# Two raw weight blocks fetched into the x buffer, later loads moved behind the first tile's last layout: a fused linear-attention and two-MLP kernel

## Chip, cores and metric

One core of a Trainium2 chip. The metric is the device time of one execution in microseconds (us). An execution is also given by its span, from the first to the last instruction of the profile.

## What is computed

Linear attention with a decaying state over 4 batches, 8 heads, 768 steps and head size 48, then two MLPs over the 3072 tokens of width 384:

```python
for t in range(S):
    state = alpha[:, :, t, :, None] * state + np.einsum('bhd,bhe->bhde', k[:, :, t], v[:, :, t])
    y[:, :, t] = np.einsum('bhd,bhde->bhe', q[:, :, t], state)
...
h = x @ w_in                                       # 384 -> 2048
g = np.maximum(h, 0.0) + alpha * np.minimum(h, 0.0)
x = g @ w_out                                      # 2048 -> 384
...
a = x @ w1                                         # 384 -> 1024
b = x @ w2
h = a * b @ w3                                     # 1024 -> 1024
return h @ w_out                                   # 1024 -> 384
```

## The kernel before

**Precision.** Each large product is made of three matmuls: every operand is held as a high part and a low part (`hi`, `lo`), and the product lo times lo is dropped. So a matrix must be split into its two parts before a matmul may read it.

**Weights.** They come as 64-bit words. Block i of 16 (`blocks[i]`, for column block f = i of the first MLP) is fetched by `fetch(i)` (L159) into a buffer `raw`, of which there are two. `convert(i)` (L163) then takes four instructions: `upper` on ScalarE writes the high half of the word to the only `top` buffer; `assemble` on VectorE joins `top` and `raw` to `y`, of which there is one buffer; `copy` on ScalarE writes the high part of weight tile `w` from `y`; a subtraction on VectorE writes its low part. `convert(i)` also issues `upper` of block i + 1, ahead of its own copy. `conv_next` (L182) calls `convert` for the next block and, one step later, `fetch(i + 2)`. The weight tiles are called w_81 (block 0), w_82 (block 1), and so on, in the listings of the order.

**Attention.** 24 chunks of 128 steps; four make one tile of 512 tokens, so there are six tiles T. For chunk n, `load(n)` fetches decays `al` (two buffers) and `qk` (two buffers), `load_v(n)` fetches `v` (three). `prep(n)` runs a scan over the decays and forms `qt` and `kn` (VectorE, with a logarithm and an exponential on ScalarE, L228 and L229, in the one buffer `r`). `chunk(n)` updates the state (`Up`, `sst`) and makes the outputs `yp`, then the masked scores of the next chunk (`scp`, `sc`). `place` (L321) carries the outputs by small DMAs into x in the layout of the MLP, for chunk 3 half of them from ScalarE's queue, half from SyncE's. `xsplit` (L335) splits half a tile of x into its parts. x has two buffers (pool `xp`).

**First MLP.** `G1(T, f)` computes `h` for a tile and a column block: 9 matmuls of 512 columns, and from it on ScalarE `u`, on VectorE `g`, on ScalarE and VectorE the two parts of `gs`. `G2(T, f)`, two steps later (LAG), adds 9 matmuls into three accumulators `acc`.

**What sets the order.** The list `first` (L441) is the program order of the attention of tile 0, with `warm_up` (matmuls on zeros that keep TensorE busy) and a clock `tick` behind each unit; `later(k, fn)` runs fn k ticks on. Behind it comes a loop over (T, f), in which each step calls `G1`, some units of the next tile's attention (`attend`), `conv_next` and `G2`. SyncE's queue follows program order (`manual_schedule`). On the other engines a scheduler moves instructions by priority. Each engine then runs its instructions in the order of the built program. All loads stand in SyncE's queue and share a few completion semaphores in turn, so that an issue also waits until an earlier DMA with its semaphore has landed.

Of the kernel before, what the change touches and what calls it, by code (L numbers as in the profile page):

```python
# [14 lines left out]
I32 = mybir.dt.int32  # L15
# [17 lines left out]
SPT = TA // CH  # L33
# [5 lines left out]
SKEW = 14  # L39
WARM0, WARM, REST = 18, 2, 18  # L40
SETTLE = 5
BEHIND = 400
BLK = 2 * DM
NSP = NJ * (3 * DM + 1024)
# [19 lines left out]
def fused_kernel(ctx, tc, qk, al, vv, wf, ws, m_alpha, ident, maskn, out):  # L64
# [58 lines left out]
    def later(k, fn):  # L123
        due.setdefault(clock[0] + k, []).append(fn)
# [6 lines left out]
    raw = {}  # L131
    top = ap1.tile([128, BLK], I32, name="top")

    def words(src, p):
        n = src.shape[1]
        t = p.tile([128, n, 2], I32, tag="raw", name="raw", bufs=2)
        sp.dma_start(out=t.bitcast(I16).rearrange("p n c -> p (n c)")[:, :4 * n - 1], in_=src.bitcast(I16)[:, 1:])
        return t

# [16 lines left out]
    blocks = [wf[f].rearrange("p o c -> p (o c)") for f in range(NF)]  # L156
    blocks += [ws[:, c:min(c + BLK, NSP)] for c in range(0, NSP, BLK)]

    def fetch(i):  # L159
        if i < len(blocks):  # L160
            raw[i] = words(blocks[i], cp)

    def convert(i, last=False):  # L163
        t = raw.pop(i)
# [17 lines left out]
    def conv_next(last=False):  # L182
        i = nconv[0]
        nconv[0] += 1
        if i < len(blocks):
            assert i + 1 in raw or i + 1 == len(blocks)
            convert(i, last)
            later(1, lambda: fetch(i + 2))

    st = {}  # L190

# [9 lines left out]
    def load_v(n):  # L201
        if n >= NSTEP:
            return
        b, c = divmod(n, NC_B)
        v = st["v", n] = ap2.tile([128, H, DP], F32, tag="v", name="v", bufs=3)
        sp.dma_start(out=v, in_=vv[b, c])

    def prep(n, last=False):
        if n >= NSTEP:
            return  # L210
        t = st.pop(("qk", n))
        P = albuf[n % 2]
        flatP = P.rearrange("p a t -> p (a t)")
        scan = dve.tensor_tensor_scan(out=flatP, data0=flatP, data1=scan1.rearrange("p a t -> p (a t)"),  # L214
                                      initial=0.0, op0=ALU.mult, op1=ALU.max)
        if last:
            tc.keep_in_program_order(scan)
        pool.memset(P[:, :, 0:1], 0.0)
        Pv = P[:, :, 1:]
        qt = ap2.tile([128, NP, CH], F32, tag="qt", name="qt")  # L220
        dve.tensor_tensor(out=qt, in0=t[:, 0], in1=Pv, op=ALU.mult)
        r = ap2.tile([128, NP, CH], F32, tag="r", name="r", bufs=1)
        kn = ap2.tile([128, NP, CH], F32, tag="kn", name="kn")
        pend = ap2.tile([128, NP, 1], F32, tag="pend", name="pend")
        pool.tensor_copy(out=pend, in_=P[:, :, CH:])
        st["pend", n], st["qt", n], st["kn", n] = pend, qt, kn

        act.activation(out=r, in_=Pv, func=AF.Ln)  # L228
        act.activation(out=r, in_=r, func=AF.Exp, scale=-1.0)  # L229
        dve.tensor_tensor(out=kn, in0=t[:, 1], in1=r, op=ALU.mult)  # L230
        dve.tensor_tensor(out=r, in0=Pv, in1=r, op=ALU.mult)
        dve.scalar_tensor_tensor(out=kn, in0=r, scalar=2.0, in1=kn, op0=ALU.subtract, op1=ALU.mult)
# [15 lines left out]
    def kT(n, w):  # L248
        if n >= NSTEP:
            return  # L250
        kn = st.pop(("kn", n))
        if ends(n):
            return
        ps = bank([128, NP, 128], "kTp", w)
        for p in range(NP):
            pe.transpose(ps[:, p], kn[:, p], idn)  # L256
        t = ap2.tile([128, NP, 128], F32, tag="kT", name="kT", bufs=1)
        copy(t, ps)
        st["kT", n] = t

    def scores(n, w):
        if n >= NSTEP:
            return
        kn, qt = st["kn", n], st["qt", n]
        ps = [bank([128, NP, CH], "scp", w) for _ in range(2)]
        for p in range(NP):
            for hh in range(2):
                r = slice(64 * hh, 64 * hh + D)
                mm(ps[hh][:, p], kn[r, p], qt[r, p], start=True, stop=True)
        for hh in range(2):  # L270
            sc = ap2.tile([128, NP, CH], F32, tag="sc", name="sc")
            dve.tensor_tensor(out=sc, in0=ps[hh], in1=msk.to_broadcast([128, NP, CH]), op=ALU.mult)  # L272
            st["sc", n, hh] = sc
# [66 lines left out]
    def chunk(n, w, more=True):  # L340
        untie()
        state(n, w)
        yout(n, w)
        if more:
            scores(n + 1, w)
        load_v(n + 3)

    def attn_units(T):
        w = T % 2
# [57 lines left out]
    with tc.manual_schedule(engines={mybir.EngineType.SP}):  # L407
# [18 lines left out]
        def warm_up(n):  # L426
            ps = pab.tile([128, 512], F32, tag="h", name="wu")
            for _ in range(n):
# [9 lines left out]
        dve.tensor_scalar(out=sgn, in0=alpha, scalar1=1.0, scalar2=-2.0, op0=ALU.is_gt, op1=ALU.mult)  # L438
        dve.tensor_scalar(out=sgn, in0=sgn, scalar1=1.0, scalar2=None, op0=ALU.add)
        dve.tensor_tensor(out=salpha, in0=alpha, in1=sgn, op=ALU.mult)  # L440
        first = [lambda: scores(0, 0), lambda: kT(0, 0), lambda: chunk(0, 0), lambda: kT(1, 0), lambda: prep(2),  # L441
                 lambda: (load(4), chunk(1, 0)), lambda: kT(2, 0), lambda: prep(3),
                 lambda: (load(5), chunk(2, 0)), lambda: kT(3, 0), lambda: conv_next(True), lambda: xsplit(0, 0, 2),
                 lambda: chunk(3, 0, False), lambda: (warm_up(REST), conv_next(True)), lambda: (prep(4, True), load(6)),
                 lambda: xsplit(0, 2, 2)]
        for u in first:
            u()
            warm_up(WARM)
# [331 lines left out]
```

## Time and profile before

| | us |
|---|---|
| median of 3 runs | 859.57 (857.78 to 859.61) |
| the profiled execution | 856.45 |
| its span | 854.7 |
| TensorE busy (matmul) | 834.7, 98% of the span |
| VectorE busy | 459.5 |
| ScalarE busy | 352.6 |
| mean granted clock of TensorE | 0.994 |

The shares are means over stages. Attention of tile 0 takes the first 32 us, the change lies between 20 and 90 us, and from about 90 us on the first MLP and all that follows it run with TensorE busy all the time until the last few microseconds. Times are counted from the start of the span.

### The profile page before, as it was taken

How to read it: one execution, taken by the hardware profiler on the slowest of the kernel's cores; microseconds unless marked ns; L12 is line 12 of the kernel's file. 1: busy time of each engine (PE TensorE's matmuls, PEld its weight loads, DVE VectorE, ACT ScalarE, POOL GpSimd, SP SyncE). 2: the span in 40 equal slices, each digit the busy share in tenths (PEclk: the TensorE clock that was granted, in tenths of full speed). 3: DMA queues.
4: the chain of work that ended last, by engine and by line, in shares of the span. 5: the costliest groups of instructions: out<-in, count | busy, mean ns of one | idle time of the engine just before them, and what ended most of it. 6: DMA issues, size and time to landing. Idle time of an engine off the chain costs nothing.

```text
span 854.7 us, 11911 instructions
## 1 busy us (share of the span) xinstructions
PE 834.7 (98%) x4772; PEld 686.0 (80%) x4776; DVE 459.5 (54%) x643; ACT 352.6 (41%) x538; POOL 11.1 (1%) x53
## 2 busy tenths in 40 slices
PE   7899999999999999999999999999999999999996
PEld 4577888888888888888888889988888888888884
DVE  7899876665685586656335634552434435322221
ACT  3567665434454545454335534522223232221221
POOL 0000000000000000000000000000000000000000
PEclk9999999999999999999999999999999999999998
DMA  7667572321673385525003306420302203010001
GB/s 279 221 202 248 181 257 97 105 79 39 227 254 106 129 297 184 184 108 196 3 18 111 123 1 224 141 79 1 134 14 74 74 25 124 1 38 1 37 1 41
DMA packets 49104, 99.56 MB, mean 116 GB/s; under 512 B 4880, under 2 KB 25488, under 8 KB 49040
## 3 DMA queue, kind: packets, MB, share of 16 engines
q1 hardware_dynamic: 48800, 98.62, 34.0%
q8 instruction: 39, 0.64, 0.3%
q14 instruction: 25, 0.20, 0.1%
q10 hardware_dynamic: 240, 0.10, 0.0%
HBM read 75.63 MB, written 18.35 MB: 110 GB/s over the span
## 4 chain that ended last, share of the span: by engine, by line
PE 91%; DVE 4%; ACT 2%; issue 1%; DMA 1%; ACTq 0%; DVEq 0%; SPq 0%
PE ab L372 23%; PE h L372 21%; PE acc L372 11%; PE acc L397 8%; PE acc L398 7%; PE acc L400 7%; PE yp L237 4%; PE w L372 4%; PE scp L237 2%; PE Up L237 1%; PE kTp L256 1%; DMA al<-in_al_dram 1%; DVE al L214 1%; DVE w L151 1%; DVE sc L272 1%
## 5 line engine op out<-in xcount | busy, mean ns | idle before, releaser
L372 PE MATMUL h<-x,w 128*128 128x512 f32 x864 | 213.8, 391 | 3.5 <-ACT x L72 3.0
L372 PE MATMUL ab<-x,w 128*128 128x512 f32 x864 | 203.6, 389 | 0.0
L372 PEld LDWEIGHTS h<-x,w 128*128 128x128 f32 x864 | 161.3, 188 | 37.9 <-ACT x L72 3.5
L372 PEld LDWEIGHTS ab<-x,w 128*128 128x128 f32 x864 | 162.1, 188 | 33.6
L397 PE MATMUL acc<-gs,w 128*128 128x512 f32 x288 | 115.4, 401 | 0.0
L398 PE MATMUL acc<-gs,w 128*128 128x512 f32 x288 | 113.1, 393 | 0.0
L576 DVE TENSOR_TENSOR c<-ab,a 128x512 f32<-128x512 f32 x48 | 33.1, 690 | 145.3 <-PE ab L372 145.3
L384 ACT ACTIVATE u<-h,sgn 128x512 f32<-128x512 f32 x96 | 65.5, 682 | 108.0 <-PE h L372 107.8
L386 DVE SCALAR_TENSOR_TENSOR g<-h,salpha,u 128x512 f32<-128x512 f32 x96 | 71.7, 747 | 68.1 <-ACT u L384 67.7
L372 PE MATMUL acc<-cs,w 128*128 128x512 f32 x432 | 105.8, 389 | 0.0
L389 DVE SCALAR_TENSOR_TENSOR gs<-g,sgn,gs 128x512 fp32r<-128x512 f32 x96 | 71.9, 749 | 51.1 <-ACT gs L388 51.0
L372 PEld LDWEIGHTS acc<-cs,w 128*128 128x128 f32 x432 | 81.0, 188 | 17.2 <-DVE cs L579 0.4
L388 ACT ACTIVATE gs<-g,sgn 128x512 fp32r<-128x512 f32 x96 | 69.1, 719 | 54.0 <-DVE g L386 54.0
L400 PE MATMUL acc<-gs,w 128*128 128x512 f32 x288 | 81.4, 391 | 0.0
L72 ACT ACTIVATE a<-ab 128x512 f32<-128x512 f32 x48 | 28.8, 599 | 109.9 <-PE ab L372 109.9
L72 ACT ACTIVATE cs<-c 128x512 fp32r<-128x512 f32 x48 | 30.2, 629 | 93.4 <-DVE c L576 93.4
L397 PEld LDWEIGHTS acc<-gs,w 128*128 128x128 f32 x288 | 54.4, 189 | 12.4 <-issue 0.2
L400 PEld LDWEIGHTS acc<-gs,w 128*128 128x128 f32 x288 | 54.5, 189 | 11.6
L398 PEld LDWEIGHTS acc<-gs,w 128*128 128x128 f32 x288 | 54.5, 189 | 10.7
L72 ACT ACTIVATE top<-raw 128x768 f16<-128x768 bf16 (+1 forms) x39 | 41.8, 1071 | 29.6 <-DMA raw<-in_ws_dram 20.8
L579 DVE TENSOR_TENSOR cs<-c,cs 128x512 fp32r<-128x512 f32 x48 | 33.2, 691 | 30.8 <-ACT cs L72 30.8
L146 DVE SCALAR_TENSOR_TENSOR y<-raw,top 128x768 int32<-128x768 int32 (+1 forms) x39 | 36.9, 947 | 7.1 <-DMA ws_d<-y 4.5
(64 smaller groups left out, 656.9 us busy)
## 6 DMA issues: line engine op xcount, KB each, us to landing
raw<-in_ws_dram SPq DMA_DIRECT2D x22, 767.8 KB, 5.1
qk<-in_qk_dram SPq DMA_DIRECT2D x24, 512.0 KB, 5.7
raw<-in_wf_dram SPq DMA_DIRECT2D x16, 767.8 KB, 4.7
ws_d<-y SPq DMA_DIRECT2D x22, 384.0 KB, 3.0
al<-in_al_dram SPq DMA_DIRECT2D x24, 256.0 KB, 4.8
v<-in_vv_dram SPq DMA_DIRECT2D x24, 256.0 KB, 4.0
alx<-in_al_dram SPq DMA_DIRECT2D x8, 768.0 KB, 4.7
x_d<-x1e SPq DMA_DIRECT2D x18, 256.0 KB, 4.3
```

The costliest lines, as they stand in the source:

```text
L72: act.activation(out=out, in_=in_, func=AF.Copy)
L146: return dve.scalar_tensor_tensor(out=y, in0=t[:, :, 0], scalar=13, in1=z[:, :n], op0=ALU.logical_shift_right, op1=ALU.bitwise_or)
L237: ins = pe.matmul(*a, **k)
L372: pe.matmul(ps, w, x, start=first and i == 0, stop=last and i == n - 1)
L384: act.activation(out=u, in_=ps, func=AF.Identity, scale=sg)
L386: dve.scalar_tensor_tensor(out=gt, in0=ps, scalar=sa, in1=u, op0=ALU.mult, op1=ALU.max)
L388: act.activation(out=s[:, 0], in_=gt, func=AF.Identity, scale=sg)
L389: dve.scalar_tensor_tensor(out=s[:, 1], in0=gt, scalar=sg, in1=f32(s[:, 0]), op0=ALU.mult, op1=ALU.subtract)
L397: pe.matmul(acc[T][m], r_out[f][:, 0, c], s[:, 0], start=f == 0, stop=False)
L398: pe.matmul(acc[T][m], r_out[f][:, 1, c], s[:, 0], start=False, stop=False)
L400: pe.matmul(acc[T][m], r_out[f][:, 0, c], s[:, 1], start=False, stop=f == NF - 1)
L579: dve.tensor_tensor(out=s[:, 1], in0=c, in1=f32(s[:, 0]), op=ALU.subtract)
```

## The change

Blocks 2 and 3 of the raw weights get a home of their own: a tile `early` in the x pool, which is x's second buffer before tile 1 needs it. They are fetched while chunks 1 and 2 run. Blocks 4 and 5 go to the `raw` buffers of blocks 0 and 1, with the fetch four ticks behind the conversion. A third block is converted in `first`; the preparation of chunk 4 moves to its end, behind the second half of x. The loads of chunk 5 and of v for chunk 6 move behind the placing of chunk 3.

```diff
+BEFORE = 4
...
-    def words(src, p):
+    def words(src, p, t=None):
         n = src.shape[1]
-        t = p.tile([128, n, 2], I32, tag="raw", name="raw", bufs=2)
+        if t is None:
+            t = p.tile([128, n, 2], I32, tag="raw", name="raw", bufs=2)
...
+    early = xp.tile([128, 2, BLK, 2], I32, tag="x", name="early")
+
     def fetch(i):
         if i < len(blocks):
-            raw[i] = words(blocks[i], cp)
+            raw[i] = words(blocks[i], cp, early[:, i - 2] if i in (2, 3) else None)
...
-            later(1, lambda: fetch(i + 2))
+            if i not in (2, 3):
+                later(BEFORE if i < 2 else 1, lambda: fetch(i + 4 if i < 2 else i + 2))
...
-        load_v(n + 3)
+        if n != SPT - 1:
+            load_v(n + 3)
...
-        first = [lambda: scores(0, 0), lambda: kT(0, 0), lambda: chunk(0, 0), lambda: kT(1, 0), lambda: prep(2),
-                 lambda: (load(4), chunk(1, 0)), lambda: kT(2, 0), lambda: prep(3),
-                 lambda: (load(5), chunk(2, 0)), lambda: kT(3, 0), lambda: conv_next(True), lambda: xsplit(0, 0, 2),
-                 lambda: chunk(3, 0, False), lambda: (warm_up(REST), conv_next(True)), lambda: (prep(4, True), load(6)),
-                 lambda: xsplit(0, 2, 2)]
+        first = [lambda: scores(0, 0), lambda: kT(0, 0), lambda: chunk(0, 0), lambda: (kT(1, 0), fetch(2)), lambda: prep(2),
+                 lambda: (load(4), chunk(1, 0)), lambda: kT(2, 0), lambda: (prep(3), fetch(3)),
+                 lambda: chunk(2, 0), lambda: kT(3, 0), lambda: conv_next(True), lambda: xsplit(0, 0, 2),
+                 lambda: chunk(3, 0, False), lambda: (warm_up(REST), conv_next(True), load(5), load_v(6)),
+                 lambda: conv_next(True), lambda: xsplit(0, 2, 2), lambda: (prep(4, True), load(6))]
```

What this does to the order on three engines follows. First ScalarE's queue, from the copy of chunk 3's output (`yT_490` before, `yT_488` now) to the copy that makes the high part of the second half of x (`x<-x`); `r<-al_109` is the logarithm of chunk 4, `w_82` and `w_83` the second and third weight tile. Before:

```order
L72 ACTIVATE yT_490<-yp 128x512
L324 DMA x<-yT_490 48x3x128
L326 DMA x<-yT_490 16x128
L326 DMA x<-yT_490 32x128
L72 ACTIVATE w_82<-y 128x2x384
L228 ACTIVATE r<-al_109 128x512
L229 ACTIVATE r<-r 128x512
L72 ACTIVATE top<-raw 128x768
L72 ACTIVATE x<-x 128x3x256
L72 ACTIVATE w_83<-y 128x2x384
```

And of the change:

```order
L73 ACTIVATE yT_488<-yp 128x512
L329 DMA x<-yT_488 48x3x128
L331 DMA x<-yT_488 16x128
L331 DMA x<-yT_488 32x128
L73 ACTIVATE top<-early 128x768
L73 ACTIVATE w_82<-y 128x2x384
L73 ACTIVATE top<-early 128x768
L73 ACTIVATE w_83<-y 128x2x384
L73 ACTIVATE x<-x 128x3x256
L233 ACTIVATE r<-al_109 128x512
```

Between the last placing DMA and the copy of x stood one weight copy, a logarithm, an exponential and one `top`; now there stand two of `top` and two weight copies, and the logarithm comes after x.

Second, VectorE in the same place, from the low part of w_81 to the low part of x's second half (before) and on to the scan of chunk 4 (now). Before:

```order
L151 TENSOR_TENSOR w_81<-y,w_81 128x2x384
L291 TENSOR_TENSOR sst_112<-tmp,pend 128x256
L146 SCALAR_TENSOR_TENSOR y<-raw,top 128x768
L151 TENSOR_TENSOR w_82<-y,w_82 128x2x384
L214 SCALAR_TENSOR_TENSOR al_109<-al_109,scan_111 128x516
L221 TENSOR_TENSOR qt<-qk,al_109 128x512
L221 TENSOR_TENSOR qt<-qk,al_110 128x512
L230 TENSOR_TENSOR kn<-qk,r 128x512
L231 TENSOR_TENSOR r<-al_109,r 128x512
L146 SCALAR_TENSOR_TENSOR y<-raw,top 128x768
L232 SCALAR_TENSOR_TENSOR kn<-r,kn 128x512
L338 TENSOR_TENSOR x<-x 128x3x256
```

And of the change:

```order
L153 TENSOR_TENSOR w_81<-y,w_81 128x2x384
L148 SCALAR_TENSOR_TENSOR y<-raw,top 128x768
L343 TENSOR_TENSOR x<-x 128x3x256
L153 TENSOR_TENSOR w_82<-y,w_82 128x2x384
L148 SCALAR_TENSOR_TENSOR y<-early,top 128x768
L153 TENSOR_TENSOR w_83<-y,w_83 128x2x384
L343 TENSOR_TENSOR x<-x 128x3x256
L219 SCALAR_TENSOR_TENSOR al_109<-al_109,scan_111 128x516
```

The scan and the products of chunk 4 left the place ahead of x, and the conversion of the third block came into it.

Third, SyncE's queue, from the placing of chunk 2 (`yT_408`) to the load of chunk 6's decays (`al_109`). Before:

```order
L324 DMA x<-yT_408 48x3x128 x2
L326 DMA x<-yT_408 32x128
L326 DMA x<-yT_408 16x128 x2
L326 DMA x<-yT_408 32x128
L137 DMA raw<-in_wf_dram 128x3071
L206 DMA v<-in_vv_dram 128x512
L324 DMA x<-yT_490 48x3x128
L326 DMA x<-yT_490 32x128
L326 DMA x<-yT_490 16x128
L137 DMA raw<-in_wf_dram 128x3071
L197 DMA al_109<-in_al_dram 128x4x128
```

And of the change:

```order
L329 DMA x<-yT_408 48x3x128 x2
L331 DMA x<-yT_408 32x128
L331 DMA x<-yT_408 16x128 x2
L331 DMA x<-yT_408 32x128
L329 DMA x<-yT_488 48x3x128
L331 DMA x<-yT_488 32x128
L331 DMA x<-yT_488 16x128
L202 DMA al_110<-in_al_dram 128x4x128
L203 DMA qk<-in_qk_dram 128x1024
L211 DMA v<-in_vv_dram 128x512
L139 DMA raw<-in_wf_dram 128x3071
```

The raw block and v no longer stand ahead of the placing of chunk 3; chunk 5's loads now stand behind it, and the load of chunk 6's decays is the next row after the last one shown.

## Rows read from the trace of the kernel before

**Rows 1.** The page: its first line, and the busy time of TensorE.

```profile
span 854.7 us, 11911 instructions
PE 834.7 (98%) x4772; PEld 686.0 (80%) x4776; DVE 459.5 (54%) x643; ACT 352.6 (41%) x538; POOL 11.1 (1%) x53
```

**Rows 2.** What TensorE's matmuls waited for in the whole span: total us, times, longest.

```profile
PE h L372 <- ACT x L72: 3.0, 1, 3.0
...
PE scp L237 <- DVE sst L287: 1.3, 1, 1.3
...
PE scp L237 <- DVE tmp L290: 0.6, 1, 0.6
PE h L372 <- DVE x L338: 0.5, 1, 0.5
```

**Rows 3.** The timeline of TensorE: start, duration, line, tiles, shape, count, and the idle time before it with what ended that. `wu` is `warm_up`.

```profile
31.18 1.09 PE L237 MATMUL yp<-qt,sst 64*64 64x128 f32 x16
32.20 5.79 PE L429 MATMUL wu<-zeros 128*128 128x512 bf16 x25
41.00 1.65 PE L372 MATMUL h<-x,w 128*128 128x512 f32 x6 [3.01 <-ACT x L72]
43.15 0.96 PE L372 MATMUL h<-x,w 128*128 128x512 f32 x3 [0.49 <-DVE x L338]
...
61.15 2.20 PE L372 MATMUL h<-x,w 128*128 128x512 f32 x9
```

**Rows 4.** The timeline of ScalarE and of its queue (ACTq: it issues a DMA).

```profile
32.32 0.60 ACT L72 ACTIVATE yT<-yp 128x512 f32<-128x512 f32 x1 [0.77 <-PE yp L237]
32.94 0.73 ACTq L324 DMA_DIRECT2D x<-yT  x1
33.71 1.25 ACTq L326 DMA_DIRECT2D x<-yT  x2
35.00 0.84 ACT L72 ACTIVATE w<-y 128x768 fp32r<-128x768 f32 x1 [2.09 <-DVE y L146]
38.01 0.63 ACT L228 ACTIVATE r<-al 128x512 f32<-128x512 f32 x1 [2.17 <-DVE al L214]
...
39.21 1.05 ACT L72 ACTIVATE top<-raw 128x768 f16<-128x768 bf16 x1
40.13 0.81 ACT L72 ACTIVATE x<-x 128x768 fp32r<-128x768 f32 x1
```

**Rows 5.** The timeline of VectorE.

```profile
33.11 0.95 DVE L146 SCALAR_TENSOR_TENSOR y<-raw,top 128x768 int32<-128x768 int32 x1
35.88 0.96 DVE L151 TENSOR_TENSOR w<-y,w 128x768 fp32r<-128x768 f32 x1 [1.82 <-ACT w L72]
36.76 1.22 DVE L214 TENSOR_TENSOR_SCAN al<-al,scan 128x516 f32<-128x516 f32 x1
...
42.15 0.95 DVE L338 TENSOR_TENSOR x<-x 128x768 fp32r<-128x768 f32 x1
...
64.30 0.96 DVE L151 TENSOR_TENSOR w<-y,w 128x768 fp32r<-128x768 f32 x1
65.30 0.96 DVE L146 SCALAR_TENSOR_TENSOR y<-raw,top 128x768 int32<-128x768 int32 x1
...
82.17 0.42 DVE L287 SCALAR_TENSOR_TENSOR sst<-Up,pend 128x256 f32<-128x256 f32 x1
```

**Rows 6.** The timeline of SyncE's queue; its duration includes the waits inside a group.

```profile
33.21 0.33 SPq L137 DMA_DIRECT2D raw<-in_wf_dram  x1
...
34.81 3.71 SPq L326 DMA_DIRECT2D x<-yT  x2
...
40.90 0.61 SPq L197 DMA_DIRECT2D al<-in_al_dram  x1
```

**Rows 7.** DMA issues in four short stretches (around 33.0, 33.2, 38.0 and 42.3 us): size, and the us from issue to landing.

```profile
x<-yT ACTq DMA_DIRECT2D x1, 72.0 KB, 5.1
...
raw<-in_wf_dram SPq DMA_DIRECT2D x1, 767.8 KB, 4.5
...
x<-yT SPq DMA_DIRECT2D x1, 8.0 KB, 1.8
...
raw<-in_wf_dram SPq DMA_DIRECT2D x1, 767.8 KB, 7.6
```

**Rows 8.** Busy time by stretch: length, then busy time and count of PE, PEld, DVE, ACT and POOL, then TensorE's granted clock (1.00 is full), DMA share and GB/s.

```profile
28.72:82.17 53.45, 48.15 (x365) 36.04 (x364) 49.95 (x69) 36.13 (x52) 3.10 (x9) 1.00 0.63 213
34.00:41.00 7.00, 3.99 (x20) 1.61 (x18) 5.08 (x8) 3.74 (x5) 1.31 (x3) 1.00 0.70 224
...
82.60:87.90 5.30, 5.26 (x28) 4.27 (x28) 5.30 (x8) 2.81 (x4) 0.19 (x1) 0.68 0.95 349
```

**Rows 9.** The timeline of TensorE around the scores of chunk 7.

```profile
80.84 0.48 PE L237 MATMUL scp<-qt,kn 48*128 48x128 f32 x2
82.64 1.16 PE L237 MATMUL scp<-qt,kn 48*128 48x128 f32 x14 [1.32 <-DVE sst L287]
83.73 0.71 PE L397 MATMUL acc<-gs,w 128*128 128x512 f32 x1
...
87.83 1.40 PE L372 MATMUL h<-x,w 128*128 128x512 f32 x5
```

**Rows 10.** The chain of waits: start, duration, what.

```profile
92.20 2.04 PE h L372 x9
```

## The prediction

> **What bounds the kernel now.** I read the page first: TensorE's matmuls fill 834.7 of a span of 854.7 us [rows 1], so the time can only come from the 20 us in which TensorE stands, from filler, or from a low clock. The list of waits then shows where it stands inside the changed stretch: 3.0 us for ScalarE's part of x, 1.3 us for a state update `sst` on VectorE, and two of about half a microsecond [rows 2]. The timeline of TensorE gives them places. Attention of tile 0 ends with the `yp` of 31.18; then come 25 filler matmuls, the wait of 3.01 us, and the first `h` of the MLP at 41.00; the fifth `h` starts at 61.15 [rows 3]. The wait for `sst` lies at 81.32 to 82.64, and what follows runs slowly: from 83.73 to 87.83 TensorE does nine `acc` matmuls and four transposes [rows 9]. Nine matmuls of that size take 2.04 us elsewhere [rows 10], and the transposes, at about 0.1 us each, some 0.4, so 4.10 us stand where 2.45 would do. In that stretch the mean granted clock was 0.68, so for a part of it the clock was at 1.2 instead of 2.4 GHz [rows 8]. Its price was 1.65 us. From 87.83 on TensorE hardly stands, so **the start of that `h`, of block 8, is the finish line**: a microsecond won or lost there is one of the whole kernel.
>
> Who holds the start of the first `h`? ScalarE's queue: placing DMAs until 34.96, the copy of w_82 at 35.00, a logarithm at 38.01 that had waited 2.17 us for a scan on VectorE, `top` at 39.21, and only then x at 40.13 [rows 4]. The landing of the last piece of x is close behind as a second holder. ScalarE's first piece, 72 KB, took 5.1 us, beside a raw block of 768 KB issued 0.27 later and landed after 4.5; the last of SyncE's pieces was held inside a group of 3.71 us [rows 6] and took 1.8 us in itself, from an issue at about 38.0 to a landing at about 39.8 [rows 7]. So the layout was late because of the raw block, but x's copy started 0.3 us after the landing, and `top` stood right ahead of it.
>
> **The placing.** With raw block and v gone from ahead of it, ScalarE's first piece should land about 2 us after its issue at 32.94 (nearest row 1.8, other bound 5.1), at 35.0. SyncE's first piece shares a completion semaphore with it, its third with ScalarE's second piece, so they are issued at about 35.0 and 36.3, and the last lands at about 38.5 to 39.0. That gains roughly 1 us, and I count it at nothing, since ScalarE now comes later than that.
>
> **ScalarE's queue ahead of x.** It now holds two `top` and two weight copies, tied to VectorE at each step. `top` of block 2 starts at 35.00 and gives way after 0.92 [rows 4]; the copy of w_82 takes 0.84, to 36.76; its low part on VectorE starts at 36.8, and the `y` of block 2 follows 1.00 behind it, as the pair at 64.30 and 65.30 does, since there is one `y` [rows 5]; it ends at 38.75. `top` of block 3 may overwrite only then: 38.8; w_83 at 39.7; x at 40.55 for 0.81; the first `h` 0.06 later, at **41.4, which is 0.4 later than now**. The low part of x ends at 42.5, ahead of the seventh matmul, so the 0.49 wait there [rows 3] goes. Two more filler matmuls end at about 38.5 and cost nothing.
>
> **41.4 to 61.** TensorE's order is now three `h` in a row, then the scores of chunk 4. The same work as between 41.00 and 61.15 stands there. Of the waits in it, 0.5 and 0.6 [rows 2] go; new ones are the state update of chunk 4, since its `kT` copy stands in ScalarE's queue behind the logarithm of chunk 5, whose scan comes late (about 1.2 us), and a bank that `g` releases (0.25). Fifth `h`: 41.4 + 20.15 - 1.1 + 1.45 = 61.9, at most 0.8 later than now.
>
> **VectorE decides the end.** From its first `y` at 28.72 to `sst` of chunk 6 at 82.17 it was busy 49.95 of 53.45 us [rows 8], so idle 3.5, of which 1.82 in the opening [rows 5]. The built order now has nearly the same set ahead of that `sst` (a `y` and a `g` more, a `qt` and a `kn` less: +0.3). But it loses more in the opening: 2.5 us for the copy of w_82 (from 34.3 to 36.8), 1.85 for that of w_83 (38.75 to 40.6), and about 1.0 for chunk 3's state and w_81 (estimate, between nothing and the 1.82 of a like wait). That is 5.4 instead of 1.8. The later 1.7 of idle need not come back, as chunk 5's decays land early now; I take 0.3, with 0 and 1.7 as the ends. `sst` then starts at 28.72 + 49.95 + 0.3 + 5.4 + 0.3 = 84.7, against 82.17, and ends at 85.1. TensorE waits for it as before, but with the nine `acc` matmuls of block 5 now ahead of the rest of the scores instead of behind. It reaches the first score of chunk 7 at about 61.9 + (80.84 - 61.15) + 0.45 = 82.0, waits for `kn` until about 83.3 (three VectorE instructions and some 2.1 us before `sst` starts, and 0.7 long), does the seven `acc` left (1.6) to 84.9, and the other scores from 85.15. Those take 7/8 of 1.09 [rows 9], the last transposes 0.35: `h` of block 8 starts at **86.45, against 87.83**.
>
> **The clock** makes the difference. Without its fall before, 87.83 would have been 86.2, and the change loses 0.3. If it stays up now, the change wins 1.4; if it falls again, it loses 0.3. I take that it stays up: dense `acc` work now lies on both sides of the wait. The nearest row is the wait of 3.01 us between filler and `h`, over which the granted clock stayed at 1.00 [rows 8]. A wait of 1.32 us behind small score matmuls was followed by the fall; so the length of a wait alone does not tell, and the other end is kept.
>
> The Trainium skill (TensorE: Matmul & The Clock Gate, Part 1) says that the window over which activity is judged runs freely and is not set back by a kernel, so that the same kernel shows a different count of slow matmuls from run to run. By that rule the fall at 83.7 would belong to one execution and its disappearance would be no gain of the change: the sum would then be +0.3. That is the first rival below. The runs shown neither prove nor exclude it; two of them differ by 1.8 us, which is about the price of one fall.
>
> **Profiled run and median.** The profiled execution took 856.45 us, 1.75 over its span; the median of the runs is 859.57, 3.1 higher. I put the difference on the median: 859.57 - 1.4 = 858.2. What a measurement of this kernel can tell from no change is about 0.2%, 1.7 us, so the forecast itself is *no difference that can be told*.
>
> **Rivals.**
> - *The clock falls again, or its fall is of the run and not of the kernel.* For it: the wait of about 1.3 us for chunk 7 remains. Against: the dense work around it. +0.3, 859.9.
> - *VectorE is no longer the bound.* If its opening idle is 2 us less than I count, `kn` of chunk 7 is ready when TensorE asks, and TensorE runs through: from 82.0 it needs 1.1 for scores, 1.6 for the `acc` left and 0.4 for transposes, so `h` of block 8 starts at 85.1, or at 84.3 if the start of the first `h` also follows the landing (38.7) by more than ScalarE's chain allows. That is -2.7 to -3.5: 856.5. Against it: the dependencies of `top`, `y` and the copies are strict, and each is priced by a row.
> - *Slower: the raw chain.* Decays of chunk 6 are loaded at 40.90 now [rows 6], when the products of chunk 4 let their buffer go. Those products come at about 47.6 in the new order, and the raw block 5 stands behind that load in SyncE's queue: issue at about 49.0, landing with 4.5 to 7.6 us [rows 7] at 53.5 to 56.6. ScalarE's queue blocks on its `top`, ahead of the copy of w_85 and of the next `gs`. The fifth `h` wants w_85 at 61.9, some 3 us behind that `top`; so a landing past about 58.5 delays TensorE one for one. If the loads of chunk 5 and block 4 ahead of it push it to 61, it costs 2.5, and no clock gain is kept: +2.8, 862.3. Against it: at least 2 us of margin.
> - *The change may not do what it says* so far as loads go ahead of the layout; here the built order shows that it does.
>
> **Chances.** Forecast 0.45 (about -0.5 to -2.2, of which 0.15 lies past -1.7 and 0.30 within), clock rival 0.22 (0.17 within, 0.05 past +1.7), TensorE-bound 0.20, raw chain 0.13. So faster 0.35, same 0.47, slower 0.18. The range takes the TensorE-bound case at its near end and some of the slow one: 855.9 to 861.4.
>
> **What would show it.** Right: first `h` at 41.2 to 41.7 with x's landing at 38.5 to 39; VectorE idle over 2 us ahead of w_82's low part; `sst` of chunk 6 two to three microseconds later than 82.17; no stretch at half clock near 84; `h` of block 8 near 86.5. Wrong: a first `h` before 40.5 (the landing was the holder), `h` of block 8 before 85.3, waits for w_85 near 61, or TensorE waits behind 90 us, where I expect none.

## The result: 0.5% slower, and in the first pair of profiles the loss lies behind the predicted finish line

| | before | after |
|---|---|---|
| median of 11 runs each (us) | 858.71 (857.41 to 859.61) | 863.33 (858.88 to 866.39) |
| ratio, with its 95% interval | | 1.0053 [1.0038, 1.0068] |
| profiled execution, its span | 856.45, 854.7 | 862.31, 860.5 |
| mean granted clock of TensorE | 0.994 | 0.992 |

The forecast was 858.2 with a range up to 861.4. The change costs 4.6 us in the median. A second set of twelve runs of the same kernel gave 863.07, ratio 1.0037 [1.0020, 1.0055]. One run of that set took 936.74 us at a granted clock of 0.849, a slow state that two runs of the kernel before also showed (1403.11 and 2158.62); the ratios and the mean clocks below leave these three out.

**What TensorE waits for.** In the list of the kernel after, which answers to [rows 2], the wait for x is as long as before, and the two small waits of the opening are gone. `kn` has three waits of 1.9 in all, the longest, 1.1, near 84, where it had been priced. One line is new: 1.8 us for `x1e`, the copy of a finished accumulator. It stood in no step of the prediction.

```profile
PE h L378 <- ACT x L73: 3.0, 1, 3.0
...
PE scp L242 <- DVE kn L237: 1.9, 3, 1.1
PE scp L242 <- ACT x1e L73: 1.8, 1, 1.8
```

**The opening went as worked out.** ScalarE's timeline of the kernel after answers to [rows 4] (start, duration, line, tiles, shape, count, and in brackets the idle time before it and what ended that). Two pairs of `top` and weight copy stand ahead of x's copy, which starts at 40.45 instead of 40.13.

```profile
34.98 1.07 ACT L73 ACTIVATE top<-early 128x768 f16<-128x768 bf16 x1 [2.11 <-DVE x L343]
35.91 0.82 ACT L73 ACTIVATE w<-y 128x768 fp32r<-128x768 f32 x1
38.80 1.06 ACT L73 ACTIVATE top<-early 128x768 f16<-128x768 bf16 x1 [2.07 <-issue]
39.72 0.82 ACT L73 ACTIVATE w<-y 128x768 fp32r<-128x768 f32 x1
40.45 0.83 ACT L73 ACTIVATE x<-x 128x768 fp32r<-128x768 f32 x1
```

VectorE's timeline answers to [rows 5]: 2.48 us of idle ahead of the low part of w_82, 1.86 ahead of that of w_83 (2.5 and 1.85 were priced), then 0.81 for the `u` of the first `h`, which wasn't priced, and the `sst` of chunk 6 at 85.68.

```profile
36.76 0.96 DVE L153 TENSOR_TENSOR w<-y,w 128x768 fp32r<-128x768 f32 x1 [2.48 <-ACT w L73]
...
40.57 0.96 DVE L153 TENSOR_TENSOR w<-y,w 128x768 fp32r<-128x768 f32 x1 [1.86 <-ACT w L73]
...
45.81 0.75 DVE L392 SCALAR_TENSOR_TENSOR g<-h,salpha,u 128x512 f32<-128x512 f32 x1 [0.81 <-ACT u L390]
...
83.57 0.67 DVE L237 SCALAR_TENSOR_TENSOR kn<-r,kn 128x512 f32<-128x512 f32 x1
...
85.68 0.41 DVE L292 SCALAR_TENSOR_TENSOR sst<-Up,pend 128x256 f32<-128x256 f32 x1
```

TensorE's timeline answers to [rows 3] and [rows 9], and goes on to where the loss is.

```profile
41.33 7.80 PE L378 MATMUL h<-x,w 128*128 128x512 f32 x27 [2.96 <-ACT x L73]
...
62.29 2.20 PE L378 MATMUL h<-x,w 128*128 128x512 f32 x9
...
84.38 0.46 PE L242 MATMUL scp<-qt,kn 48*128 48x128 f32 x2 [1.13 <-DVE kn L237]
...
135.83 1.07 PE L378 MATMUL h<-x,w 128*128 128x512 f32 x4
138.65 0.48 PE L242 MATMUL scp<-qt,kn 48*128 48x128 f32 x2 [1.75 <-ACT x1e L73]
...
139.50 1.74 PE L242 MATMUL scp<-qt,kn 48*128 48x128 f32 x14
...
141.93 1.80 PE L378 MATMUL h<-x,w 128*128 128x512 f32 x4
...
145.65 0.62 PE L378 MATMUL h<-x,w 128*128 128x512 f32 x2
```

The `h` of block 8 starts at 88.08, 0.25 later than in the kernel before. The `h` at 145.65 starts 3.69 later than its fellow, which the next fence shows at 141.96; the loss of 3.44 between them comes in one place. The same matmuls in the kernel before:

```profile
136.57 0.48 PE L237 MATMUL scp<-qt,kn 48*128 48x128 f32 x2
...
137.42 1.16 PE L237 MATMUL scp<-qt,kn 48*128 48x128 f32 x14
...
138.92 1.17 PE L372 MATMUL h<-x,w 128*128 128x512 f32 x4
...
141.96 2.20 PE L372 MATMUL h<-x,w 128*128 128x512 f32 x9
```

Read the pair so: 1.75 us are a wait for `x1e`. From the scores at 138.65 to 145.65 are 7.00 us, from 136.57 to 141.96 only 5.39, and each group inside takes longer (1.74 for 1.16, 1.80 for 1.17): 1.61 us are the clock. A further step of 1.26 comes at about 329, where TensorE waits 0.79 for a late state update, and 0.9 of the 5.9 between the two spans lies behind the last matmul.

**The clock** in the kernel after, by stretch (columns as in [rows 8]):

```profile
28.72:85.68 56.96, 51.78 (x373) 38.22 (x373) 50.02 (x69) 37.02 (x54) 2.78 (x9) 0.97 0.56 192
...
40.00:45.00 5.00, 3.67 (x10) 2.96 (x11) 4.42 (x5) 1.91 (x3) 0.78 (x2) 0.66 0.88 326
82.60:87.90 5.30, 4.17 (x27) 2.96 (x28) 5.30 (x8) 4.13 (x6) 1.23 (x2) 1.00 0.33 101
...
140.00:145.00 5.00, 5.00 (x25) 4.20 (x24) 3.12 (x5) 1.28 (x2) 0.00 (x0) 0.67 0.85 274
```

No half clock near 84, as forecast. But part of 40 to 45, behind the wait for x, and part of 140 to 145, behind the wait for `x1e`, ran at 1.2 instead of 2.4 GHz (granted 0.66 and 0.67 on the mean).

**Where the wait for x1e comes from.** SyncE's queue ahead of the load of chunk 10 (the third chunk of tile 2), in the kernel before:

```profile
122.34 0.33 SPq L178 DMA_DIRECT2D ws_d<-y  x1
122.77 0.37 SPq L137 DMA_DIRECT2D raw<-in_ws_dram  x1
123.19 1.56 SPq L197 DMA_DIRECT2D al<-in_al_dram  x1
```

And after:

```profile
120.26 0.33 SPq L182 DMA_DIRECT2D ws_d<-y  x1
120.69 0.37 SPq L139 DMA_DIRECT2D raw<-in_ws_dram  x1
123.93 0.33 SPq L182 DMA_DIRECT2D ws_d<-y  x1
124.35 0.39 SPq L139 DMA_DIRECT2D raw<-in_ws_dram  x1
124.78 0.91 SPq L202 DMA_DIRECT2D al<-in_al_dram  x1
```

`first` converts three blocks now, and the 16 steps of tile 0 still convert one each: 19 blocks instead of 18 by the end of tile 0. So one more store and one more raw block of 768 KB stand ahead of that load. A store goes out when its block is joined, some 3.7 us apart, so the load is issued 1.59 later. It also takes longer: 7.0 us to landing instead of 5.7 (the DMA view of the two stretches). The scan of chunk 10 on VectorE waits for it, and ScalarE's logarithm (`r<-al`) for the scan. In the kernel before:

```profile
128.96 1.23 DVE L214 TENSOR_TENSOR_SCAN al<-al,scan 128x516 f32<-128x516 f32 x1 [1.05 <-DMA al<-in_al_dram]
...
130.23 0.63 ACT L228 ACTIVATE r<-al 128x512 f32<-128x512 f32 x1 [0.41 <-DVE al L214]
...
135.93 1.55 ACT L72 ACTIVATE x1e<-acc 128x512 f32<-128x512 f32 x3
```

and after:

```profile
131.89 1.23 DVE L219 TENSOR_TENSOR_SCAN al<-al,scan 128x516 f32<-128x516 f32 x1 [1.45 <-DMA al<-in_al_dram]
...
133.16 0.63 ACT L233 ACTIVATE r<-al 128x512 f32<-128x512 f32 x1 [0.95 <-DVE al L219]
...
138.02 1.55 ACT L73 ACTIVATE x1e<-acc 128x512 f32<-128x512 f32 x3
```

The scan of chunk 10 is 2.93 later. Behind it and the logarithm, in VectorE's and ScalarE's order, stand `u`, `g` and `gs` of tile 1 (its column blocks 1 and 2), and behind those, in ScalarE's order, the copies `x1e`. It isn't the accumulators that are late, as some of the expectations below have it: the last `acc` matmul of tile 0 ends at 136.0 in this kernel and at 135.7 in the kernel before. ScalarE comes to copy them only at 138.02 instead of 135.93, and the scores of chunk 8 need one of their banks.

### The profile page after: what moved, and what is told of

It reads as the page before. It is cut to its first block, busy times and chain, and to the rows that moved or that the text cites. A ratio compares the mean times of both kernels' runs of the same rounds, so it can differ in the third digit from the quotient of the medians.

```text
span 860.5 us, 11912 instructions
## 1 busy us (share of the span) xinstructions
PE 838.5 (97%) x4774; PEld 687.8 (80%) x4778; DVE 458.9 (53%) x643; ACT 351.9 (41%) x538; POOL 12.9 (2%) x53
## 4 chain that ended last, share of the span: by engine, by line
PE 81%; DVE 6%; DMA 4%; issue 2%; ACT 1%; SPq 0%; DVEq 0%; ACTq 0%
PE ab L378 23%; PE h L378 18%; PE acc L378 11%; PE acc L403 6%; PE acc L404 6%; PE acc L406 6%; PE w L378 4%; PE yp L242 3%; PE scp L242 2%; DVE y L148 1%; DMA raw<-in_wf_dram 1%; DMA qk<-in_qk_dram 1%; DMA ws_d<-y 1%; PE Up L242 1%; DVE g L392 1%
## 5 line engine op out<-in xcount | busy, mean ns | idle before, releaser
L378 PE MATMUL h<-x,w 128*128 128x512 f32 x864 | 216.1, 393 | 3.0 <-ACT x L73 3.0
L73 ACT ACTIVATE top<-raw 128x768 f16<-128x768 bf16 (+1 forms) x37 | 39.7, 1072 | 31.9 <-DMA raw<-in_ws_dram 20.0
L585 DVE TENSOR_TENSOR cs<-c,cs 128x512 fp32r<-128x512 f32 x48 | 33.2, 692 | 30.9 <-ACT cs L73 30.9
L148 DVE SCALAR_TENSOR_TENSOR y<-raw,top 128x768 int32<-128x768 int32 (+1 forms) x37 | 35.0, 947 | 5.7 <-DMA ws_d<-y 4.6
```

The source lines that it names most:

```text
L73: act.activation(out=out, in_=in_, func=AF.Copy)
L148: return dve.scalar_tensor_tensor(out=y, in0=t[:, :, 0], scalar=13, in1=z[:, :n], op0=ALU.logical_shift_right, op1=ALU.bitwise_or)
L378: pe.matmul(ps, w, x, start=first and i == 0, stop=last and i == n - 1)
L585: dve.tensor_tensor(out=s[:, 1], in0=c, in1=f32(s[:, 0]), op=ALU.subtract)
```

## The experiments

Each ran in twelve runs, x_first_hold in seven, beside the kernel before on the same chip; the ratio is against those.

Theory A: the loss is the late load of chunk 10, from its place behind the extra block. Rivals: it is the changed opening; it is the extra work of converting; it is that all later conversions come one block earlier; it is the clock.

**hold_block.** The change, without the last conversion of tile 0's steps.

```diff
-            if T == 0 or 2 <= T < NTA - 1 and g % 2 == 0:
+            if T == 0 and f < NF - 1 or 2 <= T < NTA - 1 and g % 2 == 0:
```

> The changed kernel with one conversion fewer in the steps of tile 0 (none at the last column block), so that as many raw blocks stand ahead of the load of chunk 10 in SyncE's queue as before the change; the opening stays as changed. Theory A (one raw block and one store more ahead of that load make the scan of chunk 10 late on VectorE, which makes the last g, gs and copies of tile 0's accumulators late): chunk 10's decays land by about 129 instead of 131.8, no wait of TensorE at 137 (1.75 us now) and no low clock behind it, median 858 to 860. Rival B (the new opening itself, with a low clock near 41 in some runs, makes the loss): wait and fall may go, but the median stays at 862 to 864. Rival C (loads are slower throughout tiles 2 and 3): 861 to 862.

858.79 us, ratio 1.0001 [0.9986, 1.0016]. As theory A says: the scan of chunk 10 starts at 126.02, and no wait for `x1e` is left. The opening of the change, which it keeps, makes no difference that can be told (the interval is -1.2 to +1.4 us). That speaks against the opening. But the work is less as well, and later conversions come as in the kernel before; late_block below parts those two.

**before_plus_block.** The kernel before, with one conversion more between the last two steps of tile 0, and with that the extra block alone.

```diff
-            if T == 0 or 2 <= T < NTA - 1 and g % 2 == 0:
-                if T == 0:
+            if T == 0 or (T, f) == (1, 0) or 2 <= T < NTA - 1 and g % 2 == 0:
+                if T <= 1:
```

> The kernel before with one conversion more (between the last two column blocks of tile 0), so that one raw block and one store more stand ahead of the load of chunk 10; the opening is that of before. Theory A: the wait of TensorE near 137 appears, 1 to 2 us, with or without a low clock of 1.7 us behind it, median 861 to 864. Rival B: no wait, 858 to 859.5.

863.18 us, ratio 1.0048 [1.0031, 1.0066]: the whole loss, with the opening of the kernel before. TensorE's timeline of this kernel has the same wait, longer, and the same slow groups behind it:

```profile
133.31 1.07 PE L372 MATMUL h<-x,w 128*128 128x512 f32 x4
138.24 0.48 PE L237 MATMUL scp<-qt,kn 48*128 48x128 f32 x2 [3.86 <-ACT x1e L72]
...
139.38 2.07 PE L237 MATMUL scp<-qt,kn 48*128 48x128 f32 x14
```

**pin_scan.** The change, with the scan of chunk 10 held at its place in the program, so that it can't move ahead of the `g` that it stood in front of.

```diff
-                u += [lambda n=n: prep(n + 2)]
+                u += [lambda n=n: prep(n + 2, n == 2 * SPT)]
```

> The changed kernel with the scan of chunk 10 kept at its place in program order on VectorE, behind chunk 8, so that it no longer stands ahead of the last g of tile 0; the loads are those of the change. Theory A: the late landing (131 to 132) stays, but nothing of tile 0 waits for it: no wait at 137, median 858 to 860.5, with a risk of a wait for chunk 10 further on. If the landing itself slowed TensorE by another way than the scan (ScalarE's top, or a full queue), the wait stays and the median is 862 to 864.

861.43 us, ratio 1.0029 [1.0014, 1.0043], short of what was expected. The wait near 137 is gone, so it went by way of the scan; but the pinned scan also changed VectorE's later order, and a wait of 0.73 for a state update's `tmp` stands at 174 that the change doesn't have. So it doesn't tell how much the late load costs.

**x_first_hold.** hold_block with the second half of x split ahead of the third conversion in `first`, to start the first `h` earlier.

```diff
-                 lambda: conv_next(True), lambda: xsplit(0, 2, 2), lambda: (prep(4, True), load(6))]
+                 lambda: xsplit(0, 2, 2), lambda: conv_next(True), lambda: (prep(4, True), load(6))]
```

> As the first (one conversion fewer ahead of chunk 10's load), and in the opening the split of x's second half put ahead of the conversion of the third block. Theory (ScalarE's queue, not the landing, held the first h): x's copy comes behind one top and one weight copy, so the first h starts when x has landed, at about 39.6 instead of 41.3, and VectorE is less idle; median 856.5 to 859. Rival (landing or VectorE hold it anyway): first h at 41 or later, median as the first.

864.58 us, ratio 1.0050 [1.0026, 1.0074]: a miss. VectorE's timeline shows why. A scan stood ahead of x's low part (43.57) and waited for its decays:

```profile
42.42 1.23 DVE L219 TENSOR_TENSOR_SCAN al<-al,scan 128x516 f32<-128x516 f32 x1 [3.27 <-DMA al<-in_al_dram]
```

The first seven `h` matmuls started at 41.07, the others waited 1.61 for that low part, and `kn` of the next scores came 2.84 late.

**late_block.** The change with all its 19 conversions, the last one four ticks later: on SyncE's queue its store and the next raw block go behind the load of chunk 10. TensorE's order is untouched; on ScalarE and VectorE the `top`, `y`, scan and logarithm between 126 and 133 us change places.

```diff
-                if T == 0:
+                if T == 0 and f == NF - 1:
+                    later(4, conv_next)
+                elif T == 0:
                     conv_next()
```

> As the change, with all 19 blocks converted during tile 0's steps, but the last of them four ticks later, so that its store and the raw block behind it stand in SyncE's queue behind the load of chunk 10 instead of ahead of it. TensorE's order is the same as the change's. Theory A (the load of chunk 10 comes late because of its place in SyncE's queue): no wait for the copy of an accumulator near 137, chunk 10's decays landed by about 129, 858 to 860 us. Theory B (what costs is the work of the extra conversion on VectorE and ScalarE, or the opening of the change): the wait near 137 stays or moves, 862 to 864 us. Theory C (the loss is a clock that falls more often with the change, wherever it waits): no difference to the change, 863.

859.75 us, ratio 1.0016 [0.9997, 1.0035]. The work is the same, later conversions stay one block ahead, only the place differs, and most of the loss is gone: 3.3 to 3.6 us by the medians, 1.8 to 3.2 by the ratios (1.0037 and 1.0053 for the change). The remainder can't be told from nothing. SyncE's queue now shows the load ahead of the last pair:

```profile
121.87 0.63 SPq L202 DMA_DIRECT2D al<-in_al_dram  x1
...
124.67 0.33 SPq L182 DMA_DIRECT2D ws_d<-y  x1
125.09 0.38 SPq L139 DMA_DIRECT2D raw<-in_ws_dram  x1
```

Its wait for `x1e` is 0.36.

**late_fetch.** Only the raw block behind the 19th conversion goes behind the load; the store stays ahead.

```diff
-                later(BEFORE if i < 2 else 1, lambda: fetch(i + 4 if i < 2 else i + 2))
+                later(BEFORE if i < 2 else 5 if i == NF + 2 else 1, lambda: fetch(i + 4 if i < 2 else i + 2))
```

> As the change, with only the one raw block behind the 19th conversion fetched four ticks later, behind the load of chunk 10; the store of that block stays ahead of the load. Theory A in two halves: of the 2.9 us by which chunk 10's decays land later than before, about 1.6 is the later issue and 1.3 the raw block on the way at the same time. If so, the landing is at about 130.5, the wait near 137 shrinks from 1.75 to about half a microsecond, and the time is 859 to 861. If the raw block is the whole cost: 858.5. If the store ahead of the load is the whole cost, no change: 863.

860.53 us, ratio 1.0016 [0.9999, 1.0034]. By the ratio, moving the raw block alone gives back as much as moving the pair, by the median 0.8 us less; how store and block share the cost can't be told from these intervals.

**fill.** The change, with twelve filler matmuls ahead of the scores that wait.

```diff
-            u += [lambda: (untie(), scores(n0, w), kT(n0, w)), lambda: prep(n0 + 1)]
+            u += [lambda: (untie(), T == 2 and fill(12), scores(n0, w), kT(n0, w)), lambda: prep(n0 + 1)]
```

> As the change, with twelve filler matmuls (2.7 us, results unused) on TensorE ahead of the first scores of tile 2, where it waits near 137; the late load is left as it is. This leaves the wait and takes away only the idle of TensorE. If the fall of the clock behind that wait is part of the price: no stretch at half clock between 137 and 145, the start of the h of 145.65 comes about 1.7 us earlier, 861 to 862 us. If the fall comes anyway (belongs to the execution and not to the idle), or if it has no part in the medians' difference: 863 to 864, or a little more for the filler that isn't covered.

862.58 us, ratio 1.0047 [1.0027, 1.0067]. By stretch, the filler did keep the clock up:

```profile
137.00:146.00 9.00, 9.00 (x54) 6.85 (x53) 5.81 (x8) 3.72 (x8) 0.11 (x1) 1.00 0.52 175
```

and the `h` of 145.65 came at 144.27, 1.38 earlier in this execution. In the median 0.75 us are left of it, less than the intervals tell apart.

The granted clocks of all runs, in the mean, say more (they also count the microseconds behind the last matmul): 0.9929 to 0.9938 in the kernel before, 0.9924 in both sets of the change, 0.9916 in before_plus_block, 0.9942 here, 0.9951 in late_block and 0.9953 in hold_block. One thousandth is 0.86 us of 860 if TensorE works throughout. By this estimate the clock is 0.4 to 1.2 us of the loss against the kernel before, and some 2.4 us of what late_block and hold_block are faster than the change. It isn't the whole: this run, with a clock no lower than that of the kernel before, is still 4.1 us slower. Where the wait is shorter than the filler of 2.7 us, part of that is the filler.

**before_again and after_again.** Both kernels once more, unchanged.

> The kernel before, unchanged, against itself: what the measurement calls no change, and a second profiled execution. The first one took 856.45 us, some 2 us under the median of its runs, and has no wait of TensorE between 145 us and the tail, while every kernel with the new opening shows raw blocks of 7 us and more near 300 us and a state update near 327 that comes 0.3 to 0.8 late. If those late steps belong to single executions: this profile may show such blocks too, no wait near 137, 858 to 859 us. If they belong to the new opening: raw blocks of 5.5 us near 300 again and no wait there.

> The change, unchanged, a second time: median 862 to 864.5 us. Theory A, that the late load of chunk 10 is of the program and not of one execution: decays of chunk 10 landed at 131 to 132.5 again and a wait of 1 to 3 us for the copy of an accumulator near 137, with or without a fall of the clock behind it. If the wait was of that one execution: none there, and the loss sits elsewhere.

before_again: 858.99 us, ratio 0.9991 [0.9978, 1.0004]; this is what no change looks like. Its TensorE timeline corrects the picture that the first profile gave:

```profile
136.45 0.49 PE L237 MATMUL scp<-qt,kn 48*128 48x128 f32 x2 [0.99 <-ACT x1e L72]
...
139.15 2.06 PE L372 MATMUL h<-x,w 128*128 128x512 f32 x4
...
143.44 2.20 PE L372 MATMUL h<-x,w 128*128 128x512 f32 x9
```

The kernel before waits near 137 too, in this execution, and falls to half clock behind it. Its two raw blocks near 300 us took 7.2 us (median of the two) instead of 5.8, and it lost 0.86 at about 329. So the late step at 329 is not of the change alone. after_again has the wait for `x1e` again, 1.08, with no fall of the clock behind it:

```profile
139.80 0.49 PE L242 MATMUL scp<-qt,kn 48*128 48x128 f32 x2 [1.08 <-ACT x1e L73]
...
145.20 1.98 PE L378 MATMUL h<-x,w 128*128 128x512 f32 x8
```

This second pair doesn't show the loss where the first one does. From the `h` of block 8 to the `h` at 143.44 and 145.20 the kernel before takes 56.78 us and the change 55.26; in the first pair it was 54.13 and 57.57. The second profile of the change lost its time in other places, and part of it at half clock: block 8 comes at 89.94 instead of 86.66, behind falls near 14 and 42, and a third fall comes near 250, behind a wait of 1.36 for `tmp` (granted 0.57 in 14 to 18 and in 41 to 49, 0.66 in 249 to 254). So that the extra pair ahead of the load costs the time is shown by the medians of the experiments. The wait for `x1e` itself, 1.75 and 1.08 against 0 and 0.99, is 0.9 us in the mean of two profiles, and together with the clock it doesn't make up the 4.6. Where the rest lies stays open.

**skip0 and skip3.** The change with one conversion fewer at f = 0, or at f = 3, instead of at the end.

```diff
-            if T == 0 or 2 <= T < NTA - 1 and g % 2 == 0:
+            if T == 0 and f > 0 or 2 <= T < NTA - 1 and g % 2 == 0:
```

> As the change, with one conversion fewer in tile 0's steps, the one of its first step (f = 0) instead of the last as in the run hold_block: the third block converted in the opening then makes the first step's unnecessary. 18 blocks by the end of tile 0, so chunk 10's load stands where it stood before. On VectorE, the bound up to the state update of chunk 6 by the prediction, one y and one low part of a weight (1.9 us) fall out ahead of it. If VectorE bounds there as predicted: that sst starts 1.5 to 2 us earlier than the change's 85.68, the h of block 8 at 86 to 87, 856 to 857.5 us. If TensorE's own work or the weights of the next blocks take over as the bound: 858 to 859, as hold_block (858.79). If a weight comes late now that its lead is one block shorter: waits for w between 45 and 85 and over 860.

> As skip0, but the step without a conversion is the fourth (f = 3): the lead of one block is kept for three steps and given up where VectorE is busiest. 18 blocks by the end of tile 0. If the early gain of skip0 (h of block 8 at 86.6) is kept without its late weight near 91: 857 to 858.5 us. If the order of VectorE that the scheduler makes from it has other waits, as pin_scan had: 859.5 to 861.

skip0: 860.05 us, ratio 1.0017 [0.9997, 1.0036], above each time expected. `sst` of chunk 6 starts at 82.53, 3.15 earlier, but the `h` of block 8 only 1.45 earlier, at 86.63: VectorE bounded there, and as it gave way TensorE took over. The early gain isn't in the median. skip3: 860.19, ratio 1.0018 [1.0004, 1.0032]; no gain either.

**hold_rest.** hold_block with `REST` at 30 instead of 18.

> As hold_block (the change without the last conversion in tile 0's steps), with 30 instead of 18 filler matmuls behind attention of tile 0: 2.7 us more of them, which end at about 40.9, so that TensorE hardly stands ahead of the first h of 41.3. If the falls of the clock at 41 that most kernels with the new opening show come from that wait of 3 us: no half clock at 41 to 45, and 857 to 858 us. If the fall comes elsewhere instead, or the new order of TensorE and VectorE that the longer filler makes costs as much: 858.5 to 860.

861.01 us, ratio 1.0018 [1.0003, 1.0034]: a miss. The longer filler changed the order of VectorE and TensorE, and the wait moved from x to a `g`:

```profile
48.33 0.96 PE L378 MATMUL h<-x,w 128*128 128x512 f32 x3 [2.32 <-DVE g L392]
```

None of the versions beats the kernel before.

**One table for the wait.** For each profiled execution but pin_scan (whose scan was moved) and fill (whose filler covers the wait), the start of chunk 10's scan counted from its own `h` of block 8 (so that what the opening did is taken out), and the wait for `x1e` near 137:

| kernel | scan behind block 8 (us) | wait (us) | median (us) |
|---|---|---|---|
| x_first_hold | 132.84 - 94.06 = 38.78 | 0 | 864.58 |
| hold_block | 126.02 - 87.21 = 38.81 | 0 | 858.79 |
| hold_rest | 128.25 - 89.00 = 39.25 | 0 | 861.01 |
| late_block | 127.77 - 87.92 = 39.85 | 0.36 | 859.75 |
| late_fetch | 131.70 - 90.73 = 40.97 | 0 | 860.53 |
| before | 128.96 - 87.83 = 41.13 | 0 | 858.71 |
| skip0 | 128.74 - 86.63 = 42.11 | 0.22 | 860.05 |
| before_again | 129.03 - 86.66 = 42.37 | 0.99 | 858.99 |
| skip3 | 133.36 - 90.86 = 42.50 | 0.43 | 860.19 |
| after_again | 133.04 - 89.94 = 43.10 | 1.08 | 863.07 |
| after | 131.89 - 88.08 = 43.81 | 1.75 | 863.33 |
| before_plus_block | 133.03 - 85.55 = 47.48 | 3.86 | 863.18 |

Up to about 41 the scan costs nothing or little; from about 42 on the wait grows with it, though not in every row. The three executions with the extra pair ahead of the load are the last three. The kernel before sits at the edge, in its two executions on either side. The wait doesn't order the medians: x_first_hold and hold_rest have none and lose elsewhere.

## Why the prediction was wrong

- **The failed step is "From 87.83 on TensorE hardly stands, so the start of that `h`, of block 8, is the finish line".** It read one execution's lack of waits as room. The table shows that the room at the scores of chunk 8 was within a microsecond or so of nothing, and the extra block used more than that. In the first pair of profiles block 8 came 0.25 later and the `h` behind those scores 3.69 later. before_plus_block, with the old opening and the extra block, has a median 4.6 us above its kernel before; late_block gives most of the loss back by moving the pair behind the load, and hold_block, which drops it, all.
- **The order was not followed far enough.** The part on the change followed SyncE's queue up to the fifth raw block. That a third conversion in `first` makes 19 blocks by the end of tile 0, where there were 18, and that the load of chunk 10 stands behind the last of them, is in the built order and was priced at nothing, without a reason.
- **The opening.** First `h` 41.33 (41.4 predicted), low part of w_82 at 36.76 (36.8), fifth `h` 62.29 (61.9): the chain through ScalarE and VectorE up to the first `h` held. `kn` and `sst` came 1.0 later than predicted, since VectorE stood 6.9 us up to `sst` where 5.7 were counted. Most of that is the fall of the clock behind the wait for x, a term that the sum put at nothing. hold_block has the same opening and no fall there in its profile: its `sst` starts at 84.80 (84.7 predicted), its first score of chunk 7 at 83.50 (83.3), its fifth `h` at 61.36. So the nearness of 62.29 to 61.9 is luck: the waits were counted some 0.5 too high, and the fall cost 0.9.
- **Block 8** came at 88.08 instead of 86.45, in hold_block at 87.21; so 0.87 of the 1.63 go with the fall. Another 0.55 are TensorE's own work from the first score of chunk 7 on, 3.70 us where 3.15 were counted. Part of this is a misread row: the prediction took the other scores as 7/8 of 1.09, but in [rows 9] 1.09 is the time of those 14 alone. Where neither shows half clock between 28 and 90, 87.21 in hold_block stands against 86.66 in before_again, 0.55 later.
- **The clock.** It stayed up near 84, but fell behind the wait for x, the same wait whose row at full clock [rows 8] had served as the nearest sign that it would stay up. The 27 `h` took 7.80 us, in hold_block at full clock 6.72; of these 1.08, 0.9 came through to the fifth `h` and to block 8. That it stayed up near 84 is no merit of the change, and the forecast gain of 1.4, which came from there, had nothing under it. The rival that the fall at 84 is of the run and not of the kernel was right: before_again has none near 84 and one near 138. The Trainium skill, in the part named there (TensorE: Matmul & The Clock Gate, Part 1), says that the window runs freely, so that one kernel shows a different count of slow matmuls from run to run. These two traces agree, in that the fall lies near 84 in one and near 138 in the other.
- **The base.** The prediction started from the median of three runs, 859.57; over eleven it is 858.71. From that base the forecast would have been 857.3, still farther from 863.33.
- **The raw chain**, the slower rival, did not come: no wait for a weight near 61. The sign came from a mechanism that was not on the list. But the list of what would prove the prediction wrong had it: a wait of TensorE behind 90 us.

## What to carry over

- When an edit moves one step of a pipeline earlier, count how many steps the pipeline then takes in all, and look in each queue at what stands behind the last one. The cost may come 100 us behind the edit.
- A trace without a wait does not say how much room there is. Find the next wait that would open and what lies between it and zero, in more than one execution where there are more.
- Moving a transfer behind the load that is due next, with the same work done, is a small edit that tells queue order from work.

## What was not expected of the hardware

- The clock fell in different places of the same kernel: near 84 in one execution of the kernel before, near 138 in the other, each time behind a wait of about a microsecond (1.32 and 0.99). Behind the wait of 3.0 us for x it stayed up in both, and in the kernel after it fell there in both: the stretch from 40 to 46 had a granted clock of 1.00 in before and before_again, 0.72 and 0.63 in after and after_again. Over all profiles with a wait of about 3 us there, it fell in none of three with the old opening and in eight of nine with the new one, hold_block being the ninth. What in the new opening makes it more likely stays open.
- A raw block of 768 KB took 4 to 8 us, and two of them near 300 us took 5.8 us in one execution of the kernel before (median of the two) and 7.2 in the other. The cause was not looked for.
